# Decay tables by scaled exponentials, one table laid out row by row, and an operand split moved two products ahead

## The chip, the cores and the metric

One core of a Trainium2 chip runs the whole program. The metric is the device time of one execution in microseconds (us). Before the change it is 964.85 us, the median of 3 runs (964.2 to 965.12).

## What is computed

A block with adaptive layer norm: a modulation of a condition vector `c` scales and shifts two layer norms and gates two branches. The first branch is a long convolution whose kernel `K` is a sum of decaying complex exponentials (a diagonal state-space model), the second a bilinear gated unit. There are 2048 tokens, 640 channels `D`, 192 states `N` per channel, and 1536 hidden units `F`.

```python
logdA = dt * (A_re + 1j * A_im)
P = exp(logdA[:, :, None] * arange(L))          # D x N x L
K = einsum("dn,dnl,dn->dl", Cc, P, dt * Bc).real
y = irfft(rfft(pad(h)) * rfft(pad(K)))[:L] + h * Dskip
x = u + ga * y
h = layernorm(x) * (1 + cb) + sb
out = x + gb * (((h @ w_gate) * (h @ w_up)) @ w_down)
```

## The kernel before

**Stage 1 (about 0 to 430 us)** makes `K`, transforms it and the tokens, multiplies the spectra and transforms back. The 640 channels are taken in five blocks of 128. `K` is never summed term by term over `L`: an exponential at position `l` is a product of one at a coarse and one at a fine position, so for each of 40 groups (eight to a block, `n` = 0 to 39) the matrix engine multiplies a table of fine positions `P` with a table of coarse positions `Q` (L745 and L760). Each table is an amplitude times a sine or cosine. The amplitudes are `EP` (decay over fine positions) and `EQ` (decay over coarse ones, with the amplitude of the state), each an outer product that GpSimd (POOL) makes in `outer` (L649): `EP` from eight fine decays `LP` and four of the rows `RH`, `EQ` from eight values `LQ` and eight of the rows `RH`. GpSimd also makes the phases `Pha` and `Phb` on the same line. ScalarE (ACT) takes their sines into PSUM (`tra`, `trb`), and VectorE (DVE) multiplies these with `EP` and `EQ` on L731 (`PtA`, `PtB` read `EP`; `QtA`, `QtB` read `EQ`). `EP` and `EQ` have two buffers each, so that an outer product waits until the multiplication by the one before last has ended.

The decays come from a row of seeds for each block, one log decay per state, which TensorE transposes into PSUM (`ps`). The steps of a block's seeds stand in `u_seeds`, and the strings `SEG0` (first block) and `SEG` (the other four) say in which order they are recorded. Three of them matter here. `s_r` (L518) multiplies the log decay with constants: VectorE writes three multiples into `RL` (L521) and eleven into `RH` (L523), in two halves of a block. `s_e` (L535) takes exponentials on ScalarE: seven instructions with a scale of 64, 128, ... 448 write the fine decays `LP`, one runs over `RH` and one over `RL` in place. All ScalarE work goes through the helper `act` and has the line L135. `LP` is stored with the eight fine positions of a state side by side, so that each of the seven instructions writes every eighth element.

Beside the tables, the same engines do the transforms: `u_pre`, `u_g`, `u_c`, `u_d` for the tokens, the spectra, their product (L868 to L874 on VectorE) and the way back.

**Stage 2 (about 430 us to the end)** is the gated unit in two halves of the tokens. For each half, twelve steps `f` form gate and up products (`prod`, L1028) with sums of operands in the manner of a fast matrix multiplication; `y_3` and `z_2` are the last two products of a step, and VectorE, GpSimd and ScalarE combine their results. Every operand is split by `hilo` (L992) into a high part (ScalarE) and the remainder (VectorE). Then `down` (L1455) multiplies with `w_down` in twelve steps; `d_prep(tb, f)` splits that step's operands, `e` or `sl` on the token side and `wsgh`, `wsgl` on the weight side. The first two of these splits are recorded in the up loop itself, at the ends of steps 10 and 11.

**The order of the work** is written out by hand: the kernel runs under a manual schedule, each engine executes its instructions in the order in which they are recorded, and the table `SCHED` gives each piece of stage 1 the slots at which its parts are recorded. `q` in it are the slots of the seeds of the blocks after the first, one for each part of `SEG`. In stage 2 the Python loops are the order.

Of the kernel before, what the change touches and what calls it, by code (L numbers as in the profile page):

```python
# [10 lines left out]
F32 = mybir.dt.float32  # L11
F32R = mybir.dt.float32r
I32 = mybir.dt.int32
AF = mybir.ActivationFunctionType
OP = mybir.AluOpType
# [23 lines left out]
    fo=(22003, 31003, 31005, 35001),  # L39
    e0=(-87000,),  # L40
    mc=((31004, 39005, 40006, 43001, 52000), (34000, 53002, 60000, 62000, 69002), (58000, 91004, 92001)),
    q=((22004, 32000, 39001, 40005, 42006, 44000, 44001, 44002, 51000, 51001, 56001, 56002, 57000, 57002), (66002, 89000, 95003, 101000, 107000, 107001, 111000, 112000, 123000, 123003, 124001, 131000, 131003, 131004), (137001, 175000, 176001, 186009, 188001, 189001, 197003, 197004, 201000, 201001, 203002, 204001, 204002, 206001), (210002, 226000, 252005, 264003, 265002, 268001, 268002, 268003, 268005, 272001, 275000, 277000, 280002, 281001)),
    pre=(((56000, 73001, 78000), (40007, 61001, 66003), (76004, 82000, 86001), (88001, 95001, 97002)), ((119002, 127004, 132000), (131002, 131005, 135002), (86005, 99001, 100000), (118000, 118003, 118005)), ((143001, 160000, 160003), (153002, 172001, 172003), (181000, 186005, 186007), (173000, 178000, 178001)), ((221001, 252001, 252006), (224002, 242001, 242004), (245001, 261000, 261001), (281002, 281005, 285000)), ((317000, 335000, 336003), (265003, 298000, 298001), (297000, 315001, 315002), (182002, 196000, 196001))),
    c=(((161005, 162006, 165000, 166001), (122000, 122002, 154000, 155002), (144001, 144002, 167002, 168004), (125000, 125002, 141001, 141002)), ((208003, 217002, 220007, 224000), (201002, 201003, 205000, 211000), (181001, 181002, 198000, 200001), (168003, 170002, 184001, 186003)), ((292002, 295005, 308002, 308006), (245002, 249000, 253002, 253003), (254006, 256002, 278002, 281004), (291000, 291006, 302001, 303000)), ((319002, 321001, 329000, 332001), (337001, 337008, 346000, 349002), (351000, 351001, 360000, 364002), (363002, 365005, 365009, 370000)), ((375000, 379000, 391000, 392004, 393000, 403000), (386001, 386002, 392000, 393001, 394000, 404000), (380002, 385001, 388005, 392001, 392002, 392003), (365006, 371002, 392005, 396000, 398000, 404001))),
    d=(((376000, 388003, 388004), (206000, 206003, 210000), (222000, 225000, 225001), (283001, 284003, 291002)), ((236000, 244002, 248001), (251001, 261002, 262001), (267001, 270000, 270002), (224004, 240000, 244001)), ((340000, 358000, 358001), (354000, 367000, 367002), (319004, 338000, 339005), (309002, 325001, 332000)), ((397001, 401001, 409000), (406000, 414001, 414002), (402000, 414000, 431011), (411000, 424000, 431009)), ((404002, 406001, 407000, 412002), (409002, 412001, 419000, 419001), (425001, 425002, 429000, 431003), (404003, 409001, 415000, 415001))),
# [27 lines left out]
    xs='ababaaaabababa',  # L73
)
SEG0 = ("l", "a", "b", "c", "ud", "r", "x", "e", "f", "G", "g", "D", "h", "v", "R", "")
SEG = ("l", "a", "b", "c", "ud", "D", "r", "R", "x", "E", "f", "g", "h", "v")
P_PH, P_EP, P_MOD = 3, 6, 1


# [50 lines left out]
def tile_kernel(ctx: ExitStack, tc: tile.TileContext, I, out):  # L130
# [3 lines left out]
    def act(o, i, f=AF.Copy, **kw):  # L134
        return S.activation(o, i, f, **kw)  # L135
# [13 lines left out]
    sm = const.tile([P, 16], F32, name="sm")  # L149
    halfpi, dt, dt2 = sm[:, 10:11], sm[:, 0:NB], sm[:, NB : 2 * NB]  # L150
    V.memset(halfpi, math.pi / 2)
    mults = const.tile([P, 14], F32, name="mults")
    for k, m in enumerate((1536, 1024, 512, 0, 8, 16, 24, 32, 40, 48, 56, 1, 2, 4)):
        V.memset(mults[:, k : k + 1], float(m))
    shl = const.tile([P, 11], I32, name="shl")
    for k in range(11):
        V.memset(shl[:, k : k + 1], k + 1)
# [257 lines left out]
    EQ = [pk1.tile([P, 24, 64], F32, name=f"EQ{i}") for i in range(2)]  # L415
    EP = [pk1.tile([P, 24, 32], F32, name=f"EP{i}") for i in range(2)]
    LQ = pk1.tile([P, 96, 8], F32, name="LQ")
    LP = pk1.tile([P, 3, 96, 8], F32, name="LP")
    LH = pk1.tile([P, 192, 8], I32, name="LH")
    V.memset(LP[:, :, :, 0], 1.0)  # L420
    RH = pk1.tile([P, 3, 11, 96], F32, name="RH")
    RL = pk1.tile([P, 2, 4, 96], F32, name="RL")
    DH = [pk1.tile([P, 4, 192], I32, name=f"DH{i}") for i in range(3)]
    DL = [pk1.tile([P, 4, 192], I32, name=f"DL{i}") for i in range(2)]
# [3 lines left out]
    def u_seeds(db):  # L428
# [10 lines left out]
        dc = dt[:, db : db + 1]  # L439
        hs = (slice(0, 4), slice(4, 8))  # L440
        Dh, Dl = ([R[(2 * db + h) % len(R)] for h in range(2)] for R in (DH, DL))
        Rh, Rl = ([R[:, (2 * db + h) % R.shape[1]] for h in range(2)] for R in (RH, RL))

        def halves(R, hh):

            a, b = ((2 * db + h) % R.shape[1] for h in (hh[0], hh[-1]))
            return R[:, a : a + len(hh)] if a <= b else R[:, 2::-2]
# [14 lines left out]
        def free(h, *kinds):  # L462

            hf = 2 * db + h
            for k_ in kinds:
                if k_ in ("ph", "ep", "eq") and hf >= 3:
                    need(1, k_, 4 * (hf - 3) + 3)
                elif k_ in ("lh", "lq") and hf >= 2:
                    need(1, k_, hf - 2)
# [46 lines left out]
            mark("step", 2 * db + h)  # L516

        def s_r(h):  # L518
            ps = T["ps"]
            free(h, "ep", "eq", "lq")  # L520
            V.tensor_tensor(g4(Rl[h])[:, 0:3], ps[:, 0, hs[h]].unsqueeze(1).to_broadcast([P, 3, 4, 24]),  # L521
                            mults[:, 11:14].unsqueeze(2).unsqueeze(3).to_broadcast([P, 3, 4, 24]), op=OP.mult)
            V.tensor_tensor(g4(Rh[h]), ps[:, 0, hs[h]].unsqueeze(1).to_broadcast([P, 11, 4, 24]),  # L523
                            mults[:, 0:11].unsqueeze(2).unsqueeze(3).to_broadcast([P, 11, 4, 24]), op=OP.mult)

        def s_u():
            V.tensor_tensor(u, u, T["q"][:, 0], op=OP.add)
# [5 lines left out]
            V.tensor_scalar(pe[:, 1], x, 0.0, 0.5, op0=OP.is_ge, op1=OP.subtract)  # L533

        def s_e(*hh):  # L535
            lp, rh, rl = (halves(R, hh) for R in (LP, RH, RL))
            for l in range(1, 8):
                act(lp[:, :, :, l], rl[:, :, 0], AF.Exp, scale=64.0 * l)
            act(rh, rh, AF.Exp)
            act(rl[:, :, 0:3], rl[:, :, 0:3], AF.Exp)  # L540
            for h in hh:
                mark("lp", 2 * db + h)

# [34 lines left out]
        def s_v():  # L578
# [8 lines left out]
            for h in range(2):  # L587
# [1 line left out]
            mark("seeds", db)  # L589

        one = lambda f, *a: lambda: f(*a)
        steps = dict(l=s_l, a=s_a, b=s_b, c=s_c, d=one(s_d, 0), D=one(s_d, 1), r=one(s_r, 0), R=one(s_r, 1), u=s_u, x=s_x,
                     e=one(s_e, 0), E=one(s_e, 0, 1), f=s_f, G=s_G, g=s_g, h=s_h, v=s_v)
        if db == 0:
            LATE.append(lambda: s_e(1))
# [929 lines left out]
    for half in range(2):  # L1525
        i0 = half * NF
        if half == 0:

            new_s()
            new_h2()  # L1530
            H = iter(T0["hd"])
            seq = [(sums_u, 0), (x_1, 2), (x_2, 2, False), (x_c, 2), (split_u, 0, "a"), (split_u, 0, "b")]
            seq += [(tokens2, 1, 1, 0, False), (tokens2, 1, 1, 2, True), (s_sums, 0), (tokens2, 1, 1, 1, False), (tokens2, 1, 1, 3, False), (s_sums, 1)]
            seq += [(tokens2, 1, 1, 4, False), (x_1, 3), (x_2, 3, False)]
            seq += [(s_split, k, j) for j in (2, 1) for k in range(2)] + [(s_one, 4), (split_u, 0, "c"), (s_split, 0, 3), (s_split, 1, 3)]
            seq += [(s_one, 2), (s_one, 3), (s_split, 0, 4), (s_split, 1, 4), (s_five,), (x_c, 3), (sums_u, 1), (raw,), (raw_u, 2), (res_l, 0, 1)]
            seq += [(y_1, 0), (split_g, AHEAD), (z_1, 0), (y_2, 0), (split_u, 1), (sums_u, 2), (raw_u, 3), (y_3, 0), (z_2, 0), (fold, 0)]
            for g_, *a_ in seq:
                at((next(H),), once(g_), *a_)
            due(433)  # L1540
            assert not jobs
            PRE[0] = False
        else:
            for j in range(AHEAD):
                if LEAD <= j + 1 < AHEAD:
                    split_g(i0 + j + 1)
                x_1(i0 + j)
                x_2(i0 + j)
# [12 lines left out]
            res_l(3, 1)
        for f in range(1 - half, NF):
            i = i0 + f
            y_1(i)
            if f + AHEAD < NF:
                split_g(i + AHEAD)
            z_1(i)
            late = 0 < f <= NF - AHEAD
            if late:
                x_1(i + AHEAD - 1)  # L1570
            y_2(i)
            if f + 1 < NF:
                split_u(i + 1)
            if f + 2 < NF:
                sums_u(i + 2)
            if f + 3 < NF:
                raw_u(i + 3)
            if late:
                x_2(i + AHEAD - 1)
            y_3(i)  # L1580
            z_2(i)
            if half == 0:
                fold(f)
            if f >= NF - 2:
                d_prep(2 * half, f - NF + 2)
        for T in range(2):
            tb = 2 * half + T
            h2 = tb + 2 if half == 0 else None
            for f in range(NF):
                for n in (2, 3) if T == f == 0 else (f + LEAD,):  # L1590
                    if n < NF:
                        d_prep(tb, n)
                    elif T == 0:
                        d_prep(tb + 1, n - NF)
                    elif h2:
                        split_g(n)
# [26 lines left out]
```

## Time and profile before

| | |
|---|---|
| median of 3 runs | 964.85 us (964.2 to 965.12) |
| the profiled execution | 960.78 us, span 959.0 us, mean granted TensorE clock 0.978 |
| busy: PE, DVE, ACT, POOL | 863.3, 757.6, 569.7, 566.6 us |
| of these from 11.48 to 418.46 us (407.0 us): PE, DVE, ACT, POOL | 334.1, 353.4, 350.7, 385.9 us |

The profile is of one execution. Busy time is the time in which an engine had an instruction of the program in its datapath. A group row gives the line, the engine, the operation, the written and read tiles with their shapes, how many there were, their busy time and mean, and the idle time ahead of them with what ended it. A timeline row starts with start and length in us; a number in square brackets is the idle time of the engine before it, and the arrow what ended that. Ends of matrix multiplications are modelled, and ends of GpSimd work are rough.

### The profile page before, as it was taken

What the parts mean: (1) busy time and instruction counts of PE and PEld (TensorE: products, weight loads), DVE (VectorE), ACT (ScalarE), POOL (GpSimd) and SP (SyncE); (2) the same over time, 40 slices, a digit from 0 to 9 for tenths busy, and PEclk for the clock granted to TensorE, in tenths of its full rate; (3) what the DMA queues carried; (4) which work ended last, traced back from release to release, by engine and by line L of the source; (5) the groups of instructions that cost most, each with busy time, mean ns of one, the idle gap of its engine ahead of it and who ended that gap; (6) DMA issues with size and microseconds to landing.
All of it is one profiled execution on the core that took longest, in us unless ns stands there. A gap on an engine that the chain in (4) does not pass through costs nothing.

```text
span 959.0 us, 26424 instructions
## 1 busy us (share of the span) xinstructions
PE 863.3 (90%) x11070; PEld 715.4 (75%) x11070; DVE 757.6 (79%) x1328; ACT 569.7 (59%) x1022; POOL 566.6 (59%) x419
## 2 busy tenths in 40 slices
PE   2878876898798689889889999999999999999998
PEld 1565655676675467678568888889998888889998
DVE  8998688888889988888899777786677877687452
ACT  6899988887987879754773322225555322223330
POOL 5999999799799999940135866721021544451000
PEclk9977999999999899999999999999999999999999
DMA  8487575434455655478854355155536222212241
GB/s 304 150 289 243 164 222 194 138 112 129 139 183 157 178 148 159 126 228 245 234 157 121 99 192 180 40 192 165 193 137 219 84 83 82 83 55 84 82 166 55
DMA packets 141320, 148.94 MB, mean 155 GB/s; under 512 B 8208, under 2 KB 119568, under 8 KB 139792
## 3 DMA queue, kind: packets, MB, share of 16 engines
q1 hardware_dynamic: 139904, 145.80, 48.4%
q8 instruction: 87, 1.43, 0.6%
q10 hardware_dynamic: 1296, 1.44, 0.5%
q14 instruction: 33, 0.27, 0.1%
HBM read 108.36 MB, written 38.86 MB: 154 GB/s over the span
## 4 chain that ended last, share of the span: by engine, by line
PE 46%; DVE 6%; issue 1%; ACT 1%; POOL 1%; DMA 0%; SPq 0%; DVEq 0%; ACTq 0%
PE pa L1028 26%; PE pa L1455 17%; PE psg L1028 1%; DVE sl L992 1%; DVE wtl L992 0%; PE psg L1108 0%; DMA TVb<-WD 0%; PE psg L1455 0%; DVE a L1147 0%; DVE wsgl L992 0%; ACT hfb L135 0%; PE psg L1162 0%; DVE st L1081 0%; DVE xb L1468 0%; DVE hl L1149 0%
## 5 line engine op out<-in xcount | busy, mean ns | idle before, releaser
L649 POOL TENSOR_TENSOR EQ<-LQ,RH 128x1536 f32<-128x1536 f32 x40 | 124.1, 3103 | 1.1 <-DVE QtB L731 1.1
L135 ACT ACTIVATE z<-pa 128x512 f32<-128x512 f32 x24 | 14.3, 598 | 167.6 <-PE pa L1028 114.7
L992 DVE TENSOR_TENSOR wsgl<-wga,wsgh 128x640 fp32r<-128x640 f32 x72 | 67.6, 943 | 46.5 <-ACT wsgh L135 46.5
L135 ACT ACTIVATE wsgh<-wga 128x640 fp32r<-128x640 f32 x72 | 52.3, 732 | 66.5 <-PE pa L1455 30.2
L1399 POOL TENSOR_TENSOR z<-z,s 128x512 f32<-128x512 f32 x24 | 33.4, 1390 | 88.6 <-DVE s L1398 88.6
L1004 POOL TENSOR_TENSOR tf<-wur,wgb 128x256 f32<-128x256 f32 x24 | 18.8, 782 | 99.6 <-DVE wtl L992 58.9
L649 POOL TENSOR_TENSOR EP<-LP,RH 128x768 f32<-128x768 f32 x40 | 65.7, 1650 | 11.6 <-DVE PtB L731 11.5
L1455 PE MATMUL pa<-wsgh,sh 128*128 128x384 f32 (+1 forms) x295 | 68.6, 311 | 0.0
L1455 PE MATMUL pa<-wsgl,sh 128*128 128x384 f32 (+1 forms) x295 | 68.2, 310 | 0.0
L1455 PE MATMUL pa<-wsgh,sl 128*128 128x384 f32 (+1 forms) x295 | 68.2, 310 | 0.0
L649 POOL TENSOR_TENSOR Pha<-LH,DH 128x1536 int32<-128x1536 int32 (+1 forms) x21 | 62.4, 2971 | 1.3 <-ACT tra L135 1.1
L649 POOL TENSOR_TENSOR Phb<-LH,DH 128x1536 int32<-128x1536 int32 x20 | 62.2, 3112 | 0.0
L992 DVE TENSOR_TENSOR wtl<-tf,wth 128x256 fp32r<-128x256 f32 (+1 forms) x72 | 58.8, 843 | 0.0
L731 DVE TENSOR_TENSOR QtA<-tra,EQ 128x1024 f32<-128x1024 f32 x44 | 51.8, 1214 | 8.0 <-POOL LQ L643 3.2
L1397 DVE TENSOR_TENSOR s<-pa,s 128x512 f32<-128x512 f32 x24 | 16.6, 690 | 42.9 <-PE pa L1028 37.9
L731 DVE TENSOR_TENSOR QtA<-trb,EQ 128x1024 f32<-128x1024 f32 x36 | 42.7, 1215 | 9.6 <-ACT trb L135 3.9
L760 PE MATMUL kg<-QtB,PtB 64*32 64x64 f32 x2560 | 45.3, 220 | 4.3 <-issue 2.2
L760 PEld LDWEIGHTS kg<-QtB,PtB 64*32 64x32 f32 x2560 | 38.4, 108 | 11.8 <-issue 5.9
L1028 PE MATMUL pa<-sh,wtl 128*128 128x512 f32 x144 | 44.6, 391 | 0.9 <-DVE wtl L992 0.9
L1455 PEld LDWEIGHTS pa<-wsgh,sl 128*128 128x128 f32 x295 | 45.3, 188 | 0.0
L1455 PEld LDWEIGHTS pa<-wsgh,sh 128*128 128x128 f32 x295 | 45.3, 188 | 0.0
L1455 PEld LDWEIGHTS pa<-wsgl,sh 128*128 128x128 f32 x295 | 45.3, 188 | 0.0
(653 smaller groups left out, 2854.5 us busy)
## 6 DMA issues: line engine op xcount, KB each, us to landing
wga<-wdg SPq DMA_DIRECT2D x24, 640.0 KB, 4.3
wga<-B_w_gate SPq DMA_DIRECT2D x12, 640.0 KB, 5.9
wgb<-B_w_gate SPq DMA_DIRECT2D x24, 320.0 KB, 3.3
wur<-B_w_up SPq DMA_DIRECT2D x24, 320.0 KB, 4.0
xb<-x2d SPq DMA_DIRECT2D x6, 1280.0 KB, 8.6
t_ti<-w_mod SPq DMA_DIRECT2D x3, 1600.0 KB, 8.6
t_tw<-w_mod SPq DMA_DIRECT2D x3, 1600.0 KB, 9.5
WD<-Wa SPq DMA_DIRECT2D x8, 512.0 KB, 3.7
```

Of the source, the lines that this page charges most:

```text
L135: return S.activation(o, i, f, **kw)
L649: G.tensor_tensor(o.rearrange("p x (h l) -> p x h l", l=8), lo.unsqueeze(2).to_broadcast([P, rows, nh, 8]), hi.rearrange("p h x -> p x h") ...
L731: V.tensor_tensor(t, tr, e.unsqueeze(1).to_broadcast([P, 2, R, 32]), op=OP.mult)
L760: PE.matmul(kg[j * 32 : j * 32 + 32, dd, :], PtB[lo : lo + 64, c, r, :], QtB[lo : lo + 64, c, r, :], start=False, stop=dd == 7 and c == 1, ...
L992: V.tensor_tensor(lo, v, hi, op=OP.subtract)
L1004: G.tensor_tensor(t[:, 0:2], u[:, 0:2], g[:, 0:2], op=OP.subtract)
L1028: PE.matmul(ps, w[a][:, k], x[b][:, l], start=n == 0 and m == 0, stop=n == 2 and m == len(ks) - 1)
L1397: V.tensor_tensor(S67[i], ps, S6[i], op=OP.add)
L1399: G.tensor_tensor(ZT[i], ZT[i], S67[i], op=OP.add)
L1455: PE.matmul(ACC[tb][t][c], x[:, ts], w[:, cs], start=st, stop=f == NF - 1 and n == 2 and (one or t % 2 == 1))
```

## The change

It has two parts that do not touch each other.

The first is in stage 1. `s_r` no longer multiplies by constants: it copies the log decay once into row 0 of `RL`, for both halves of a block in one instruction (`S`; in the first block in two, `r` and `R`). `s_e` makes every decay directly, as an exponential of this row with a constant scale: seven for `LP`, ten for `RH`, three for `RL`, the last of them in place. Row 3 of `RH`, whose exponent is 0, is set to 1 once at the start. The tile of constants `mults` goes. `LP` is stored the other way round, eight rows of 96 states, so that ScalarE writes it side by side, and `mk_ep` hands GpSimd a view of it in the old order, in which neighbouring elements lie 96 elements (384 bytes) apart. The waits for the readers of the old `RH` move from `s_r` to `s_e`.

The second is in stage 2: in step 11 of each half the split for the second down step is recorded ahead of `y_3` and `z_2` and no longer behind them.

On VectorE, in the fourth block's seeds (`psfa` is the bank with the transposed log decay). Before:

```order
L731 TENSOR_TENSOR PtAa<-trb,EP_143 128x1024
L521 TENSOR_TENSOR RL<-psfa,mults 128x288
L523 TENSOR_TENSOR RH<-psfa,mults 128x1056
L521 TENSOR_TENSOR RL<-psfa,mults 128x288
L523 TENSOR_TENSOR RH<-psfa,mults 128x1056
L731 TENSOR_TENSOR PtB<-tra,EP_143 128x512
L731 TENSOR_TENSOR QtB<-tra,EQ_141 128x16x32 x2
```

With the change:

```order
L733 TENSOR_TENSOR PtAa<-trb,EP_128 128x1024
L520 COPY RL<-psfa 128x2x96
L733 TENSOR_TENSOR PtB<-tra,EP_128 128x512
L733 TENSOR_TENSOR QtB<-tra,EQ_126 128x16x32 x2
L529 TENSOR_SCALAR psfc<-ptb 128x192
```

Four instructions ahead of `PtB` became one. On ScalarE, in the same block's `s_e`, before:

```order
L135 ACT_TABLE_LOAD
L135 ACTIVATE LP<-RL 128x192 x7
L135 ACTIVATE RH<-RH 128x2112
L135 ACTIVATE RL<-RL 128x2x288
L135 ACT_TABLE_LOAD
```

With the change:

```order
L135 ACT_TABLE_LOAD
L135 ACTIVATE LP<-RL 128x2x96 x7
L135 ACTIVATE RH<-RL 128x2x96 x10
L135 ACTIVATE RL<-RL 128x2x96 x3
L135 ACT_TABLE_LOAD
```

Nine instructions became twenty, at the same place. On VectorE in step 11 of the first half (the `s` are the results of the up products, L1416 and L1405 those of `y_3` and `z_2`). Before:

```order
L1398 TENSOR_TENSOR s_8714<-z,s_8714 128x512
L1416 TENSOR_TENSOR s_8735<-psg,s_8735 128x512
L1405 TENSOR_TENSOR s_8714<-psg,s_8714 128x512
L1410 TENSOR_TENSOR a_7468<-a_7468,s_8714 128x512
L992 TENSOR_TENSOR e<-a_7456,e 128x512
L992 TENSOR_TENSOR wsgl<-wga,wsgh 128x640
```

With the change:

```order
L1400 TENSOR_TENSOR s_8752<-z,s_8752 128x512
L994 TENSOR_TENSOR e<-a_7494,e 128x512
L994 TENSOR_TENSOR wsgl<-wga,wsgh 128x640
L1418 TENSOR_TENSOR s_8773<-psg,s_8773 128x512
L1407 TENSOR_TENSOR s_8752<-psg,s_8752 128x512
L1412 TENSOR_TENSOR a_7506<-a_7506,s_8752 128x512
```

The pair of splits moved ahead of three combinations. On TensorE, GpSimd and SyncE no instruction moves, and on ScalarE none besides those of `s_e`.

```diff
-SEG = ("l", "a", "b", "c", "ud", "D", "r", "R", "x", "E", "f", "g", "h", "v")
+SEG = ("l", "a", "b", "c", "ud", "D", "S", "x", "E", "f", "g", "h", "v")
...
-    mults = const.tile([P, 14], F32, name="mults")
-    for k, m in enumerate((1536, 1024, 512, 0, 8, 16, 24, 32, 40, 48, 56, 1, 2, 4)):
-        V.memset(mults[:, k : k + 1], float(m))
...
-    LP = pk1.tile([P, 3, 96, 8], F32, name="LP")
+    LP = pk1.tile([P, 3, 8, 96], F32, name="LP")
     LH = pk1.tile([P, 192, 8], I32, name="LH")
-    V.memset(LP[:, :, :, 0], 1.0)
     RH = pk1.tile([P, 3, 11, 96], F32, name="RH")
+    V.memset(LP[:, :, 0], 1.0)
+    V.memset(RH[:, :, 3], 1.0)
...
         def s_r(h):
-            ps = T["ps"]
-            free(h, "ep", "eq", "lq")
-            V.tensor_tensor(g4(Rl[h])[:, 0:3], ps[:, 0, hs[h]].unsqueeze(1).to_broadcast([P, 3, 4, 24]),
-                            mults[:, 11:14].unsqueeze(2).unsqueeze(3).to_broadcast([P, 3, 4, 24]), op=OP.mult)
-            V.tensor_tensor(g4(Rh[h]), ps[:, 0, hs[h]].unsqueeze(1).to_broadcast([P, 11, 4, 24]),
-                            mults[:, 0:11].unsqueeze(2).unsqueeze(3).to_broadcast([P, 11, 4, 24]), op=OP.mult)
+            for i in h:
+                free(i, "lq")
+            rl = RL[:, 0:2, 0].rearrange("p h (s r) -> p h s r", r=24)[:, h[0] : h[-1] + 1]
+            V.tensor_copy(rl, T["ps"][:, 0, hs[h[0]].start : hs[h[-1]].stop].rearrange("p (h s) r -> p h s r", s=4))
...
         def s_e(*hh):
+            for h in hh:
+                free(h, "ep", "eq")
             lp, rh, rl = (halves(R, hh) for R in (LP, RH, RL))
             for l in range(1, 8):
-                act(lp[:, :, :, l], rl[:, :, 0], AF.Exp, scale=64.0 * l)
-            act(rh, rh, AF.Exp)
-            act(rl[:, :, 0:3], rl[:, :, 0:3], AF.Exp)
+                act(lp[:, :, l], rl[:, :, 0], AF.Exp, scale=64.0 * l)
+            for k in (2, 1, 0):
+                act(rh[:, :, k], rl[:, :, 0], AF.Exp, scale=512.0 * (3 - k))
+            for k in range(4, 11):
+                act(rh[:, :, k], rl[:, :, 0], AF.Exp, scale=8.0 * (k - 3))
+            for k in (2, 1, 0):
+                act(rl[:, :, k], rl[:, :, 0], AF.Exp, scale=float(2**k))
...
-        outer(EP[n % 2], LP[:, hf % 3, r], RH[:, hf % 3, 3::-1, r], 24, 4, OP.mult)
+        outer(EP[n % 2], LP[:, hf % 3, :, r].rearrange("p l x -> p x l"), RH[:, hf % 3, 3::-1, r], 24, 4, OP.mult)
...
+            if f == NF - 1:
+                d_prep(2 * half, 1)
             y_3(i)
             z_2(i)
             if half == 0:
                 fold(f)
-            if f >= NF - 2:
-                d_prep(2 * half, f - NF + 2)
+            if f == NF - 2:
+                d_prep(2 * half, 0)
```

In the table `SCHED`, the row `q` loses one slot for each of the four later blocks, since `S` takes the place of `r` and `R`.

More of the change, by code (lines that the diff above doesn't have):

```diff
@@ L41 @@
     mc=((31004, 39005, 40006, 43001, 52000), (34000, 53002, 60000, 62000, 69002), (58000, 91004, 92001)),
-    q=((22004, 32000, 39001, 40005, 42006, 44000, 44001, 44002, 51000, 51001, 56001, 56002, 57000, 57002), (66002, 89000, 95003, 101000, 107000, 107001, 111000, 112000, 123000, 123003, 124001, 131000, 131003, 131004), (137001, 175000, 176001, 186009, 188001, 189001, 197003, 197004, 201000, 201001, 203002, 204001, 204002, 206001), (210002, 226000, 252005, 264003, 265002, 268001, 268002, 268003, 268005, 272001, 275000, 277000, 280002, 281001)),
+    q=((22004, 32000, 39001, 40005, 42006, 44000, 44001, 51000, 51001, 56001, 56002, 57000, 57002), (66002, 89000, 95003, 101000, 107000, 107001, 111000, 123000, 123003, 124001, 131000, 131003, 131004), (137001, 175000, 176001, 186009, 188001, 189001, 197003, 201000, 201001, 203002, 204001, 204002, 206001), (210002, 226000, 252005, 264003, 265002, 268001, 268002, 268005, 272001, 275000, 277000, 280002, 281001)),
     pre=(((56000, 73001, 78000), (40007, 61001, 66003), (76004, 82000, 86001), (88001, 95001, 97002)), ((119002, 127004, 132000), (131002, 131005, 135002), (86005, 99001, 100000), (118000, 118003, 118005)), ((143001, 160000, 160003), (153002, 172001, 172003), (181000, 186005, 186007), (173000, 178000, 178001)), ((221001, 252001, 252006), (224002, 242001, 242004), (245001, 261000, 261001), (281002, 281005, 285000)), ((317000, 335000, 336003), (265003, 298000, 298001), (297000, 315001, 315002), (182002, 196000, 196001))),
@@ L441, in u_seeds @@
         Dh, Dl = ([R[(2 * db + h) % len(R)] for h in range(2)] for R in (DH, DL))
-        Rh, Rl = ([R[:, (2 * db + h) % R.shape[1]] for h in range(2)] for R in (RH, RL))
+        Rl = [RL[:, h] for h in range(2)]
         def halves(R, hh):
@@ L591, in u_seeds @@
         one = lambda f, *a: lambda: f(*a)
-        steps = dict(l=s_l, a=s_a, b=s_b, c=s_c, d=one(s_d, 0), D=one(s_d, 1), r=one(s_r, 0), R=one(s_r, 1), u=s_u, x=s_x,
+        steps = dict(l=s_l, a=s_a, b=s_b, c=s_c, d=one(s_d, 0), D=one(s_d, 1), r=one(s_r, (0,)), R=one(s_r, (1,)), S=one(s_r, (0, 1)), u=s_u, x=s_x,
                      e=one(s_e, 0), E=one(s_e, 0, 1), f=s_f, G=s_G, g=s_g, h=s_h, v=s_v)
```

## The prediction, made before the run

> **What bounds the kernel now.** I read the page first for the span, then the busy time by stretch and the waits of GpSimd in the stretch that the first part of the change touches, and then the chain of work that ended last.
>
> ```profile
> span 959.0 us, 26424 instructions
> core 0: us, PE busy (x) PEld busy (x) DVE busy (x) ACT busy (x) POOL busy (x), PEclk, DMA share, GB/s
> 11.48:418.46 406.98, 334.13 (x7494) 252.71 (x7496) 353.36 (x575) 350.65 (x610) 385.90 (x240) 0.95 0.57 177
> ```
>
> From GpSimd's first table work (11.48) to the end of its last amplitude table (418.46) GpSimd is busy for 385.9 of 407.0 us, 95%. VectorE and ScalarE are at 87% and 86%, TensorE at 82%. So whatever leaves VectorE in this stretch leaves an engine that has 54 us to spare, and whatever lands on GpSimd lands on one that has 21. Its waits there, with the three long ones by place:
>
> ```profile
> POOL EP L649 <- DVE PtB L731: 11.5, 3, 6.3
> POOL Pha L649 <- ACT tra L135: 1.1, 1, 1.1
> POOL EQ L649 <- DVE QtB L731: 1.1, 1, 1.1
> POOL LQ L643 <- DVE RL L571: 0.9, 2, 0.5
> POOL DL L585 <- POOL ptb L584: 0.7, 1, 0.7
> ...
> 173.78 1.65 POOL L649 TENSOR_TENSOR EP<-LP,RH 128x768 f32<-128x768 f32 x1 [4.37 <-DVE PtB L731]
> ...
> 252.42 1.66 POOL L649 TENSOR_TENSOR EP<-LP,RH 128x768 f32<-128x768 f32 x1 [6.27 <-DVE PtB L731]
> ...
> 333.94 3.26 POOL L649 TENSOR_TENSOR EP<-LP,RH 128x768 f32<-128x768 f32 x2 [0.89 <-DVE PtB L731]
> ```
>
> That is 15.3 us of real waiting, 10.6 of it at two places, both ended by VectorE freeing an `EP` buffer. The other 6 us or so are gaps between instructions, which come with their number. After the stage TensorE sets the end:
>
> ```profile
> 638.09 41.92 PE pa L1455 x284
> ...
> 870.57 45.05 PE pa L1455 x307
> ```
>
> These are two of the long pieces of the chain; from 638 us on it is almost nothing but such pieces. What shifts the end of stage 1 shifts the start of this, and so the end, one for one.
>
> **The change part by part.** *VectorE's multiples.* They leave, and a copy comes.
>
> ```profile
> L523 DVE TENSOR_TENSOR RH<-psfa,mults x6: 1244/1244/1244, 147.2 to 331.7; 128x1056 f32<-128x1056 f32 x6
> L521 DVE TENSOR_TENSOR RL<-psfa,mults x6: 444/444/444, 146.8 to 331.3; 128x288 f32<-128x288 f32 x6
> L571 DVE COPY RL<-psfa x4: 247/252/256, 92.6 to 339.9; 128x96 f32<-128x96 f32 x4
> ```
>
> A later block had two pairs, 2 x (1.24 + 0.44) = 3.38 us. The first two rows give 1.04 ns an element, so the copy of 192 takes about 0.25 + 0.10 = 0.35 (an estimate from the copy of 96). That frees 3.03 us in each of four blocks, and 2 x (1.69 - 0.25) = 2.9 in the first: 15.0 us of VectorE. It reaches GpSimd only where GpSimd waits behind these instructions. That is one place above all, the wait of 6.27 us, where the freeing `PtB` stands right behind the four instructions:
>
> ```profile
> 251.60 0.68 DVE L731 TENSOR_TENSOR PtB<-tra,EP 128x512 f32<-128x512 f32 x1
> ...
> 249.38 0.60 ACT L135 ACTIVATE tra<-ab 128x512 f32<-128x512 f32 x1
> ```
>
> The `PtB` could start 3.0 us earlier, but it reads the cosine that ScalarE ends at 249.98. So it gains 1.6 us, not 3.0; ScalarE is late next. At 173.78 the four instructions are over 20 us back, and VectorE has waited for ScalarE in between: I take nothing there.
>
> *ScalarE's exponentials.* Nine instructions become twenty. Rows of one later block:
>
> ```profile
> 162.83 0.36 ACT L135 ACTIVATE ptb<-ptb 128x192 f32<-128x192 f32 x1
> 163.10 0.32 ACT L135 ACTIVATE psfc<-ptb 128x192 f32<-128x192 f32 x1
> ...
> 164.72 2.70 ACT L135 ACTIVATE LP<-RL 128x192 f32<-128x192 f32 x7
> ...
> 169.07 0.67 ACT L135 ACTIVATE RL<-RL 128x576 f32<-128x576 f32 x1
> ```
>
> The old set took from 164.72 to 169.74, 5.02 us. Side by side, 192 elements follow each other after 0.27 us, so twenty take 19 x 0.27 + 0.36 = 5.5: +0.5 us a later block. Writing `LP` side by side pays for most of the eleven more. In the first block's two sets the same eleven cost at most 11 x 0.27 = 3.0 us each, less what the shorter `RH` saves; GpSimd has other tables to make then. ScalarE is not the fullest engine and I take 0 of this for the path; uncovered it is up to 4 x 0.5 = 2 us from the later blocks. The wait for the readers of the old `RH` moves from VectorE's queue to ScalarE's, ahead of the sines queued there; there are three rings of `RH`, the readers ended half a block earlier, and no row shows VectorE waiting for them. Nothing.
>
> *GpSimd's strided read.* No instruction is added, but 40 of them read `LP` in another way, and this is the largest term.
>
> ```profile
> L649 POOL TENSOR_TENSOR EP<-LP,RH 128x768 f32<-128x768 f32 x40 | 65.7, 1650 | 11.6 <-DVE PtB L731 11.5
> ...
> L634 POOL TENSOR_TENSOR LH<-LH,DL 128x192 int32<-128x192 int32 x9 | 6.2, 690 | 0.7
> L628 POOL TENSOR_TENSOR DH<-DH 128x192 int32<-128x192 int32 x9 | 5.3, 593 | 0.0
> ...
> L609 POOL TENSOR_TENSOR LQ<-LQ,RL 128x192 f32<-128x192 f32 x10 | 5.6, 559 | 0.8
> ```
>
> L634 and L628 are the same size. L628 reads two operands side by side; L634 reads one of its two at every eighth element, 32 bytes apart. The difference is 97 ns over 192 elements, 0.5 ns an element. L609 reads one operand in side-by-side pairs that lie 32 bytes apart and writes with that jump too, at 559: a jump at every second element costs nothing visible. `EP` after the change jumps 384 bytes at every element, like L634 and unlike L609. So the price of the jump is 768 x 0.505 = 0.39 us, `EP` 2.04 us, 40 of them +15.5 us. Bounds: nothing (+0), if the broadcast second operand of `EP`, which L634 does not have, leaves room for it; and 768 x 690/192 = 2.76 us at most, +44 us, if the whole of L634 with its fixed part counted by element, which is too much. A more sensible upper end adds half as much again, 0.6 us each, +24. I take 0.39, the difference of the nearest pair.
>
> [...]
>
> How much of +15.5 us reaches the end depends on where the tables stand between the waits:
>
> ```profile
> 11.48:92.99 81.51, 11.24 (x12) 13.12 (x8) 0.85 0.73 254
> 92.99:173.78 80.79, 14.85 (x16) 11.46 (x7) 0.98 0.57 181
> 173.78:252.42 78.64, 15.18 (x16) 11.53 (x7) 1.00 0.48 138
> 252.42:333.94 81.52, 15.10 (x16) 13.14 (x8) 0.94 0.57 167
> 333.94:418.46 84.52, 16.36 (x17) 16.46 (x10) 0.98 0.49 143
> ```
>
> (The second bracket is the number of `EP` made in each stretch.) The first three stretches hold 22, +8.6 us, against about 2.7 + 4.4 + 6.3 = 13.4 us of waits. These waits take it all. At 252.42 GpSimd leaves when `PtB` frees the buffer, 1.6 us earlier by the above, less what the later tables have cost VectorE on the way, which I put at 0.7: -0.9. The last two stretches hold 18, +7.0 us, against 0.9 + 1.1 us of waits: +5.0. Sum for GpSimd at its end: +4.1 us. Its readers have a little slack there:
>
> ```profile
> 406.01 3.11 POOL L649 TENSOR_TENSOR EQ<-LQ,RH 128x1536 f32<-128x1536 f32 x1
> ...
> 410.56 2.36 DVE L731 TENSOR_TENSOR QtA<-tra,EQ 128x1024 f32<-128x1024 f32 x2 [0.48 <-ACT Wa L135]
> ```
>
> That table ends at 409.12 and is read at 410.56, 1.4 us, and two `EP` (0.8 us) still come after it. So VectorE's last stretch, which ends the stage, is later by 4.1 - 2.2 = **+1.9 us**.
>
> *The split moved ahead.* At the first `down` of the first half:
>
> ```profile
> 634.08 0.69 DVE L1416 TENSOR_TENSOR s<-psg,s 128x512 f32<-128x512 f32 x1 [1.41 <-POOL z L1399]
> ...
> 636.62 0.68 DVE L992 TENSOR_TENSOR e<-a,e 128x512 fp32r<-128x512 f32 x1
> 637.22 0.81 DVE L992 TENSOR_TENSOR wsgl<-wga,wsgh 128x640 fp32r<-128x640 f32 x1
> ...
> 637.35 0.56 PE L1455 MATMUL pa<-wsgh,e 128*128 128x384 f32 x2 [0.91 <-DVE e L992]
> 638.09 0.56 PE L1455 MATMUL pa<-wsgl,e 128*128 128x384 f32 x2 [0.17 <-DVE wsgl L992]
> ```
>
> TensorE waits 0.91 and 0.17 us for the pair. The pair takes about 1.35 us from start to end of the datapath and now fits into the 1.41 us in which VectorE waited for GpSimd's `z`, so L1416 and what is queued behind it keep their time. Gain 0.91 + 0.17 = **-1.1 us**. In the second half no row shows TensorE waiting there: 0. If VectorE's idle time were not there, three combinations would be 1.4 us later, and no product reads them soon.
>
> **Sum:** +1.9 - 1.1 = +0.8 us on the span of 959.0. The profiled execution took 960.78 us and the median is 964.85, 4.1 above it; I carry the change over: 965.7, said as **966 us**.
>
> **The rivals.** *The strided read is free* (for it: L609's pairs and the broadcast operand; against it: L634). Then GpSimd leaves 252.42 with -1.6, loses the waits of 0.9 and perhaps 1.1 behind it, and the stage ends 2.5 to 3.6 us earlier; with -1.1 that is 960 to 961.5 us, faster.
>
> *GpSimd's read costs more and rules the stage* (slower side): at 0.6 us each the first three stretches have 13.2 us against 13.4, the last two 10.8 - 2.0 = +8.8, less 1.4 + 1.2 of slack, less 1.1: +5.1, 970 us. For it: a jump of 384 bytes is wider than L634's 32. It decides from where the price passes 0.45 us. [...]
>
> *ScalarE is late next.* At 249.38 it already holds up VectorE; +0.5 us in four blocks on the path, and the first block's, add 2 to 3 us: 968 to 969. Against it: its 86%.
>
> **How the numbers follow.** No change can be told from this measurement within 0.2%, 1.9 us. My forecast 0.45, with a range of its own of 963 to 969, since the 0.7 and the slack can be off by 2 or 3 us (faster 0.04, same 0.24, slower 0.17). Free read 0.30 (faster 0.28, same 0.02). Dearer read 0.17, of it 0.05 for the rule's size. ScalarE 0.08 (same 0.03, slower 0.05). Together faster 0.32, same 0.29, slower 0.39. The range of 959 to 973 reaches over the free read and over the middle of the dearer one.
>
> **What would show it.** The `EP` group's mean first: 2.04, or 1.65, or 2.3 and more. GpSimd's waits for `PtB` shrunk at 173.78 and 252.42, its busy time in the stretch up by 15 us. ScalarE's set of a later block at 5.5 us. TensorE's waits for `e` and `wsgl` at the first `down` gone. I am wrong if VectorE's 15 us show in the stage's length, or if `EP` keeps its mean and the stage is no shorter.

## The result

The changed kernel takes 971.2 us (median of 6 runs, 970.14 to 973.48), the kernel before 964.2 us beside it (6 runs, 962.89 to 965.12). The ratio is 1.0079, 95% interval 1.0063 to 1.0096: slower. 966 was forecast, with a range of 959 to 973 and 0.39 for slower. So the time lies in the range, but on the side of the rivals.

The profiled execution after took 970.89 us, span 969.1 us, against 960.78 and 959.0 before. GpSimd's groups and waits in stage 1 after the change (the same columns as in the prediction):

```profile
L651 POOL TENSOR_TENSOR EP<-LP,RH 128x768 f32<-128x768 f32 x40 | 83.8, 2101 | 4.8 <-DVE PtB L733 4.8
...
POOL EP L651 <- DVE PtB L733: 4.8, 2, 2.8
...
POOL LQ L645 <- DVE RL L573: 1.4, 1, 1.4
...
176.97 2.11 POOL L651 TENSOR_TENSOR EP<-LP,RH 128x768 f32<-128x768 f32 x1 [2.81 <-DVE PtB L733]
...
254.55 2.09 POOL L651 TENSOR_TENSOR EP<-LP,RH 128x768 f32<-128x768 f32 x1 [2.04 <-DVE PtB L733]
```

`EP` takes 2.10 us, 0.45 more; the waits for `PtB` fell from 11.5 to 4.8 us, but did not go. In their place other engines wait for GpSimd: VectorE for `EQ` and ScalarE for `Pha`. Before, VectorE has no wait for `EQ` at all and ScalarE this one for `Pha`:

```profile
ACT PtAb L135 <- POOL Pha L649: 4.3, 3, 2.1
```

After:

```profile
DVE QtA L733 <- POOL EQ L651: 7.0, 7, 2.4
...
ACT PtAb L135 <- POOL Pha L651: 8.1, 5, 3.2
```

This is no accident of one trace. In the four kernels of this document whose GpSimd makes all 40 `EP` at 2.10 us, ScalarE's wait is 7.5 to 10.1 us and VectorE's 5.0 to 10.0; in the eight that make them at 1.65, it is 3.5 to 4.6 and at most 2.1.

The place at 252.42 us, where VectorE's relief was to reach GpSimd, on ScalarE and VectorE after the change:

```profile
249.49 1.06 ACT L135 ACTIVATE PtAb<-Pha 128x1024 f32<-128x1024 int32 x1 [0.54 <-POOL Pha L651]
...
252.28 0.35 DVE L520 COPY RL<-psfa 128x192 f32<-128x192 f32 x1
253.72 0.69 DVE L733 TENSOR_TENSOR PtB<-tra,EP 128x512 f32<-128x512 f32 x1 [1.08 <-ACT tra L135]
```

The four multiples are one copy, and `PtB` now waits for the cosine, as forecast. But the cosine itself is late: `PtB` starts at 253.72 and not at 251.60. Ahead of it ScalarE waited for GpSimd's phases (`Pha`, at 249.49); that wait is 0.54 us, so it is only a part of the delay.

ScalarE's set of a later block, and TensorE at the first `down`:

```profile
167.91 1.88 ACT L135 ACTIVATE LP<-RL 128x192 f32<-128x192 f32 x7
169.69 2.62 ACT L135 ACTIVATE RH<-RL 128x192 f32<-128x192 f32 x10
172.22 0.99 ACT L135 ACTIVATE RL<-RL 128x192 f32<-128x192 f32 x3
...
641.04 0.68 DVE L994 TENSOR_TENSOR e<-a,e 128x512 fp32r<-128x512 f32 x1
641.64 1.92 DVE L994 TENSOR_TENSOR wsgl<-wga,wsgh 128x640 fp32r<-128x640 f32 x1
643.49 0.68 DVE L1418 TENSOR_TENSOR s<-psg,s 128x512 f32<-128x512 f32 x1
```

The set takes 5.3 us (167.91 to 173.21). The second pair of splits (641.04 and 641.64) runs ahead of L1418, and TensorE, which reaches its product at 644.7, has no wait there. The pair takes 2.5 us, though, and not the 1.35 of the prediction: `wsgl`, which now runs while GpSimd makes `z`, takes 1.92 us in place of 0.81.

What the forecast did not have at all stands in the last two stages. The chain of waits holds pieces of the same number of the same matmuls in both kernels, before (with the piece at 870.57 that the prediction shows) and after:

```profile
503.60 105.73 PE pa L1028 x465
...
726.76 139.73 PE pa L1028 x615
...
952.99 2.48 DVE xb L1468 x6
```

```profile
734.39 140.55 PE pa L1030 x615
...
879.02 45.92 PE pa L1457 x307
...
963.11 2.48 DVE xb L1470 x6
```

615 matmuls of the up loop, a mix of shapes, take 0.82 us longer, 1.3 ns each; 307 of `down` take 0.87 us longer, 2.8 ns each. The groups of `down` by shape say the same, before and after:

```profile
L1455 PE MATMUL pa<-wsgh,sl 128*128 128x384 f32 x148 | 50.0, 338 | 0.0
...
L1455 PE MATMUL pa<-wsgh,sl 128*128 128x256 f32 x139 | 38.8, 279 | 0.0
```

```profile
L1457 PE MATMUL pa<-wsgh,sl 128*128 128x384 f32 x147 | 50.1, 341 | 0.0
...
L1457 PE MATMUL pa<-wsgh,sl 128*128 128x256 f32 x140 | 39.5, 282 | 0.0
```

The granted clock is 1.00 in both from 640 us on. No line of the diff touches these instructions. What it does touch is the list of tiles: the table `mults`, 56 bytes a partition, is gone, and in the built program the tiles that are laid out behind it from the same end of the memory begin 64 bytes lower. `wsgh` began at byte 45536 of a partition, 96 over a multiple of 128, and begins at 45472, 32 over one; `wsgl` moves with it. `sh` and `sl` are laid out from the other end and keep their address. So in these groups only one operand has moved, the one that TensorE streams (`wsgh` or `wsgl`, 256 or 384 columns); the one of 128 by 128 that it holds has not. That became a theory of its own, beside two others: that GpSimd paces stage 1, so that the dearer read is paid; and that ScalarE's twenty exponentials are.

### The profile page after: what moved, and what is told of

It reads as the page before. It is cut to its first block, busy times and chain, and to the rows that moved or that the text cites. A ratio compares the mean times of both kernels' runs of the same rounds, so it can differ in the third digit from the quotient of the medians.

```text
span 969.1 us, 26463 instructions
## 1 busy us (share of the span) xinstructions
PE 867.6 (90%) x11070; PEld 718.8 (74%) x11070; DVE 747.2 (77%) x1301; ACT 573.0 (59%) x1088; POOL 585.4 (60%) x419
## 4 chain that ended last, share of the span: by engine, by line
PE 48%; DVE 4%; ACT 1%; issue 1%; DVEq 0%; ACTq 0%
PE pa L1030 28%; PE pa L1457 16%; PE psg L1030 1%; DVE st L1083 1%; DVE sl L994 1%; PE psg L1164 1%; PE psg L1110 0%; PE psg L1457 0%; PE psfc L829 0%; PE psfa L829 0%; DVE a L1149 0%; ACT hh L135 0%; PE psfb L829 0%; ACT xb L135 0%; DVE xb L1470 0%
## 5 line engine op out<-in xcount | busy, mean ns | idle before, releaser
L994 DVE TENSOR_TENSOR wsgl<-wga,wsgh 128x640 fp32r<-128x640 f32 x72 | 70.8, 987 | 47.4 <-ACT wsgh L135 47.4
L651 POOL TENSOR_TENSOR EP<-LP,RH 128x768 f32<-128x768 f32 x40 | 83.8, 2101 | 4.8 <-DVE PtB L733 4.8
```

What stands on the lines that cost most here:

```text
L651: G.tensor_tensor(o.rearrange("p x (h l) -> p x h l", l=8), lo.unsqueeze(2).to_broadcast([P, rows, nh, 8]), hi.rearrange("p h x -> p x h") ...
L994: V.tensor_tensor(lo, v, hi, op=OP.subtract)
```

## The experiments

Each run stands beside runs of the kernel before on the same chip. Those had medians of 964.2, 964.2, 964.1 and 962.6 us in the four groups of runs, and single runs scatter over 7 to 11 us. One trace is worse than a median for stage 1. In the trace of part 2 alone the code up to 500 us is that of before, word for word, and yet TensorE is 5 us later at that point. Four traces with the stage 1 of before come to it at 503.6, 505.7, 508.5 and 510.7 us. In this one the granted clock was 0.79 for 8 us, which may be a part of it. Before, and part 2 alone (TensorE, weight load, VectorE, ScalarE, GpSimd, then the clock):

```profile
432.00:440.00 8.00, 8.00 (x174) 7.48 (x168) 5.21 (x13) 5.43 (x11) 0.00 (x0) 1.00 1.03 330
```

```profile
432.00:440.00 8.00, 5.46 (x72) 3.79 (x73) 0.81 (x2) 2.32 (x5) 0.00 (x0) 0.79 0.89 301
```

From 503 us on, in contrast, traces of equal code agree within 0.1 us. So I take the part behind this point (503 us before, where the long piece of the up loop begins) from the traces, and stage 1 from the medians less that part.

**Each part alone, and the layout alone.** Part 2 alone moves `d_prep(2 * half, 1)` in the kernel before; part 1 alone leaves it where it was. Expected for part 2 alone:

> Part 2 alone on the kernel before. Pacemaker theory (GpSimd's table reads cost the time, part 2 saves what it was said to): TensorE's waits of 0.91 and 0.17 us for e and wsgl at the first down are gone, 964.2 - 1.1 to 1.3 = about 963.0 us. Rival (ScalarE theory) says nothing else of this part. If the move costs VectorE something later, 964 or more.

Measured 963.39 against 964.22 us, ratio 0.9989 (0.9966 to 1.0013): the median as expected, the interval holds no change as well. Its trace has 1.6 us less behind 503 us. For part 1 alone:

> Part 1 alone. Both theories: the 7.0 us of the whole change plus the 1.1 to 1.3 that part 2 gives, 964.2 + 8.2 = about 972.4 us, with EP at 2.10 us. If the two parts are not additive, it differs from this by more than 1 us.

971.41 us, ratio 1.0083 (1.0056 to 1.0109), 1 us under the expectation: the two parts add up within what can be measured.

Then the layout without the rest, and the rest without the layout:

```diff
-    LP = pk1.tile([P, 3, 96, 8], F32, name="LP")
+    LP = pk1.tile([P, 3, 8, 96], F32, name="LP")
...
-                act(lp[:, :, :, l], rl[:, :, 0], AF.Exp, scale=64.0 * l)
+                act(lp[:, :, l], rl[:, :, 0], AF.Exp, scale=64.0 * l)
...
-        outer(EP[n % 2], LP[:, hf % 3, r], RH[:, hf % 3, 3::-1, r], 24, 4, OP.mult)
+        outer(EP[n % 2], LP[:, hf % 3, :, r].rearrange("p l x -> p x l"), RH[:, hf % 3, 3::-1, r], 24, 4, OP.mult)
```

> Only the layout: LP row by row and read at the jump, with VectorE's old multiples and ScalarE's nine old instructions, no part 2. Pacemaker theory: EP at 2.10 us, GpSimd + 18 us less the waits that swallow some 10 to 13 of it: + 7 to + 10 us, 971 to 974 us. Rival (ScalarE): the waits of GpSimd swallow nearly all, ScalarE has nine instructions as before, 964 to 967 us.

969.09 us, ratio 1.0053 (1.0035 to 1.0071): 4.9 us for the layout, less than the theory's 7 and more than ScalarE's would have. `EP` took 2.10 us:

```profile
L649 POOL TENSOR_TENSOR EP<-LP,RH 128x768 f32<-128x768 f32 x40 | 83.7, 2102 | 5.8 <-DVE PtB L731 5.8
```

The whole change with these three lines turned back:

> The whole change, but LP keeps its old layout: ScalarE writes it at a jump of 32 bytes, GpSimd reads it side by side. Pacemaker theory: EP back at 1.65 us, 40 x 0.45 = 18 us leave GpSimd, VectorE's relief and part 2 are all that is left: stage 1 ends 2.5 to 3.6 us earlier than before, the whole 959 to 961 us. Rival (ScalarE is late next): ScalarE has all twenty exponentials and its set of a later block is longer still (some 6 us against 5.3), so the time stays at 968 to 972 us though EP is short.

967.9 us, ratio 1.0039 (1.0019 to 1.0059), though `EP` was back at 1.66 us. By the expectation that was ScalarE's theory, and it seemed to stand: its set took 6.0 us a block. To see it alone, the next run gave VectorE its multiples back (nobody reads them) and left ScalarE with the twenty:

> Only ScalarE's twenty exponentials in place of nine, LP in its old layout, VectorE still makes all multiples (nobody reads them), no part 2. Against the run with the old layout this gives VectorE its 15 us back. Theory 1 (VectorE's relief is worth nothing, ScalarE's longer set, 6.0 against 5.0 us, stands on the path): 967.9 + 0.8 for part 2 = 968 to 969.5 us. Theory 2 (VectorE's relief is worth the 2.5 to 3.6 us of the prediction, ScalarE costs all the more): 971 to 972.5 us. Theory 3 (ScalarE costs nothing, the old layout was slow for another reason): 964 us.

965.81 us, ratio 1.0018 (1.0000 to 1.0036). That fits none of the three, and is 2 us less than the run with the old layout, in which VectorE had 15 us less to do. A relief that costs time was the contradiction that led to the matmul rows: 338 ns here, where the table `mults` is still there, 341 ns in the run with the old layout, where it is gone.

**The addresses.** The whole change, with an unused tile of 64 bytes where the table lay:

```diff
+    pad = const.tile([P, 16], F32, name="pad")
+    V.memset(pad[:, 0:1], 0.0)
     shl = const.tile([P, 11], I32, name="shl")
```

> The whole change plus an unused tile of 64 bytes a partition where the table of multiples lay, so that every tile behind it has its old address again. Theory of addresses (the matmuls of the last stages that stream wsgh and wsgl take 282 and 341 ns in place of 279 and 338 in every kernel without the table, and in none with it): 279 and 338 ns again, 2.9 us of TensorE back, 971.2 - 2.9 = 968.3 us. Rival (those 3 ns come from the granted clock or from another part of the change): 282 and 341 ns stay, 971 us.

966.47 us, ratio 1.0018 (1.0000 to 1.0037), 4.7 us less than the change without the tile, where 2.9 were expected. Its rows have the old times:

```profile
L1459 PE MATMUL pa<-wsgl,sh 128*128 128x384 f32 x152 | 51.4, 338 | 0.0
...
732.56 139.75 PE pa L1032 x615
...
876.38 45.05 PE pa L1459 x307
...
958.80 2.48 DVE xb L1472 x6
```

And the other way round, in the kernel before: the same table, taken from another pool, so that the tiles of the last stages begin 64 bytes lower and the tables of stage 1 stay where they are. All instructions are those of before; the constants are written one place later.

```diff
-    mults = const.tile([P, 14], F32, name="mults")
+    mults = pk1.tile([P, 14], F32, name="mults")
```

> The kernel before, with nothing changed but the place of the table of multiples: it lies behind the constants, so that the tiles of the last stages (wsgh, wsgl and others) begin 64 bytes lower, as after the change, while LP, RH and the tables of stage 1 stay where they are. Theory of addresses: 282 and 341 ns for the matmuls that stream wsgh and wsgl, 2.9 us more, 967 us. Rival (the 64 bytes matter only together with the change): 279 and 338 ns, 964.1 us.

967.2 against 962.64 us, ratio 1.0061 (1.0037 to 1.0086). The rows:

```profile
L1455 PE MATMUL pa<-wsgh,sl 128*128 128x384 f32 x151 | 51.5, 341 | 0.0
...
505.66 106.51 PE pa L1028 x465
...
730.38 140.51 PE pa L1028 x615
...
874.97 45.92 PE pa L1455 x307
...
959.05 2.48 DVE xb L1468 x6
```

From the piece at 503.60 to the last combination: 952.99 - 503.60 = 449.4 us before, 959.05 - 505.66 = 453.4 us here. So 64 bytes cost 4.0 us, in a kernel whose arithmetic and order are untouched. This theory stands. A start on the 128-byte line itself was tried too, with an unused tile of 32 bytes and part 2:

> Part 2 alone plus an unused tile of 32 bytes a partition ahead of the others: wsgh and its neighbours then begin at a multiple of 128 bytes (before: 96 over one; after the change: 32 over one). Theory of addresses: the matmuls' time changes with it, and since the sign for this place is not known from any run, 279 ns or less and 963.4 us or less if a start on the 128-byte line is the best place, some 282 ns and 966.3 us if it is like 32 over. Rival (addresses do not matter): 279 ns and 963.4 us, nothing moved.

963.01 us, ratio 0.9991 (0.997 to 1.0012), not to be told from part 2 alone. The products of `down` take 279 and 336 ns, no more than before. Other products like this place less: in its trace the first 549 matmuls of the up loop take 125.76 us, against 124.98 in part 2 alone and 125.69 in the change, and the whole way behind 503 us is 448.7 us, 0.9 more than with part 2 alone. So the 128-byte line is no better place for all of them together.

**The read.** The whole change, in which GpSimd takes the eight rows as if they lay in the old order, and so the wrong elements:

```diff
-        outer(EP[n % 2], LP[:, hf % 3, :, r].rearrange("p l x -> p x l"), RH[:, hf % 3, 3::-1, r], 24, 4, OP.mult)
+        lp = LP[:, hf % 3].rearrange("p l x -> p (l x)").rearrange("p (x l) -> p x l", l=8)
+        outer(EP[n % 2], lp[:, r], RH[:, hf % 3, 3::-1, r], 24, 4, OP.mult)
```

> The whole change, but GpSimd reads the row-by-row LP as if it lay in the old order, side by side; this leaves the right choice of LP's elements out, and the time of the read alone is changed: EP back at 1.65 us. It is the world of the rival of the prediction, the free read. Theory 1 (GpSimd's 18 us cost what they cost alone, 5 us): 971.2 - 5 = about 966 us, of which 2.9 are the addresses. Theory 2 (ScalarE's set rules, as with the old layout): 968 to 971 us. The prediction's own price for this world: 971.2 less 5 to 6 us.

965.6 us, ratio 1.0018 (1.0004 to 1.0032): 5.6 us less than the change, all by the read. The first theory holds.

The read by itself, in a kernel of nothing else:

> A small kernel that leaves the whole computation out and only times reads, four of each, nothing beside them on the other engines: GpSimd's EP product of 768 elements with LP at a step of 4, 8, 16, 32 and 384 bytes, then with LP and RH taken row by row (24 side by side in both), with the result side by side and with a jump of 128 bytes; VectorE's product of 1024 with EP side by side and at a step of 96 bytes; ScalarE's exponential of 192 written side by side and at a step of 32 bytes. Theory 1 (the price is the jump itself, the same from 8 or 16 bytes up): 1.65 us at 4, 2.10 at all steps from 8 or 16 on. Theory 2 (the price grows with the distance): 1.65, then rising, with 32 bytes clearly under 2.10 and 384 at 2.10. Row by row on both sides: 1.65 if only the operand's jump counts. ScalarE 0.27 against 0.38 us a piece.

The tiles `step__69`, `step__74`, `step__79`, `step__84` and `step__89` are the steps of 4, 8, 16, 32 and 384 bytes, `rowsin__94` the product row by row. Some of the sums of VectorE that end the small kernel did run beside GpSimd, against the expectation's "nothing beside them". Rows with no VectorE beside them:

```profile
10.69 1.64 POOL L50 TENSOR_TENSOR step__69<-big,hi 128x768 f32<-128x768 f32 x1
12.29 1.66 POOL L50 TENSOR_TENSOR step__74<-big,hi 128x768 f32<-128x768 f32 x1
...
22.18 1.97 POOL L50 TENSOR_TENSOR step__79<-big,hi 128x768 f32<-128x768 f32 x1
24.11 2.00 POOL L50 TENSOR_TENSOR step__84<-big,hi 128x768 f32<-128x768 f32 x1
...
42.56 2.09 POOL L50 TENSOR_TENSOR step__89<-rows,hi 128x768 f32<-128x768 f32 x1
44.61 1.78 POOL L50 TENSOR_TENSOR rowsin__94<-rows,hi 128x768 f32<-128x768 f32 x1
```

A step of 8 bytes took 0.02 us more than one of 4 (1.66 against 1.64), one of 16 took 0.33 us more (20%), one of 384 took 0.45 more (27%): in these rows a cliff between 8 and 16 bytes and a slight slope behind it, so each theory had half. Row by row it took 1.78 us, where 1.65 was expected if only the operand's jump counts.

**VectorE's relief.** By the working of the prediction a free read was to bring 2.5 to 3.6 us, from VectorE's relief. Alone (copy for multiples, ScalarE with nine instructions on constants, the table kept):

> VectorE's relief alone: the copy in place of the multiples, ScalarE with its nine instructions in the old layout, the unused table kept for the addresses, no part 2. RH and the rest of RL are taken as constants (ScalarE exponentiates zero times their contents), so the powers are left out of the result; the instructions of stage 1 are otherwise as before. By the prediction's working, with EP unchanged the stage ends 2.5 to 3.6 us earlier: 960.5 to 961.6 us. Ring theory (the old layout against the exponentials alone gave 0.0 us once 2.9 us for the addresses and 0.8 us for part 2 are taken out): within 1 us of 964.1.

963.62 against 962.64 us, ratio 0.9997 (0.9975 to 1.0018): nothing that can be measured, and the forecast gain lies outside the interval. GpSimd sets the constants first, so its tables begin 0.3 us later here. Its waits show where the relief went:

```profile
POOL EP L651 <- DVE PtB L733: 10.6, 3, 5.9
...
POOL LQ L645 <- DVE RL L573: 3.4, 3, 1.9
POOL Pha L651 <- ACT tra L135: 2.1, 1, 2.1
```

The waits for `PtB` gave up 0.9 us (11.5 before), those for the next amplitudes grew by 2.5 (0.9 before) and for a `tra` by 1.0 (1.1 before). In the three other traces with the stage 1 of before, these are 11 to 13, 1.3 to 1.6 and 0.8 to 1.0 us, so the two that grew are clear of the scatter. GpSimd reaches the amplitudes sooner than they are ready: VectorE's copy of them (`RL`, L573) itself waits 3.7 us for TensorE in this trace.

**Products moved to VectorE.** A try for a faster kernel: if GpSimd paces the stage and VectorE has room, 11 `EP` belong on VectorE.

> Part 2 alone, with 11 of the 40 EP products made by VectorE in place of GpSimd (old layout, old multiples). VectorE's price is estimated at 0.86 us each (768 elements at 1.04 ns and some 0.06), + 9.5 us for VectorE, - 18 us for GpSimd. Theory 1 (GpSimd paces stage 1, VectorE has room): 2 to 4 us less than part 2 alone, 959.5 to 961.5 us. Theory 2 (stage 1 hangs on a ring of all engines, and what one sheds is waited for at the next): 963 us. Theory 3 (VectorE's queue is in the way): 965 us or more.

973.55 us, ratio 1.0098 (1.0074 to 1.0123), 10 us more than part 2 alone, as the third theory has it. My price was wrong: not 0.86 but 1.48 us each, from 0.95 to 2.38.

```profile
L649 DVE TENSOR_TENSOR EP<-LP,RH 128x768 f32<-128x768 f32 x11 | 16.3, 1482 | 0.0
...
143.50 0.95 DVE L649 TENSOR_TENSOR EP<-LP,RH 128x768 f32<-128x768 f32 x1
202.18 2.38 DVE L649 TENSOR_TENSOR EP<-LP,RH 128x768 f32<-128x768 f32 x1
```

VectorE got 16 us more, put into a queue on which every product waits. So its 54 us to spare are not there when they are wanted, and 16 us more cost much where 15 us less had brought nothing.

No kernel that was tried beats the one before by more than the measurement tells. Part 2 alone takes 1.6 us less by its trace, under a fifth of a per cent.

## Why the prediction was right and wrong

The medians put together, each as the difference to the kernel before on its chip (us). The middle column is by the method of the address run, from the beginning of the long piece of the up loop (503 us before) to the last combination.

| run | whole | behind 503 us, by the trace | stage 1, the rest |
|---|---|---|---|
| the change | +7.0 | +2.4 | +4.6 |
| part 1 alone | +7.2 | +4.0 | +3.2 |
| the change, old addresses | +2.4 | -1.6 | +4.0 |
| layout alone | +4.9 | 0 | +4.9 |
| the change, read side by side | +1.5 | +2.4 | -0.9 |
| the change, old layout | +3.7 | +2.4 | +1.3 |
| VectorE's relief alone | +1.0 | 0 | +1.0 |
| exponentials alone, old layout | +1.6 | 0 | +1.6 |
| part 2 alone | -0.8 | -1.6 | +0.8 |
| before, shifted by 64 bytes | +4.6 | +4.0 | +0.6 |

The last two have the stage 1 of before, and should read 0 in the last column; they read 0.8 and 0.6. The intervals of the ratios are wider, 1.3 to 2.5 us to either side of each row, so differences of 1 or 2 us between single rows tell nothing.

- *The read.* Forecast 2.04 us an `EP`, measured 2.10; forecast 4.4 to 5.5 us of time between the free read and the dear one, measured 4.6 + 0.9 = 5.5 between the change and the read side by side. This step held: the nearest pair of rows said 0.39 us an `EP`, the upper end of half as much again 0.6, and 0.45 was measured. The 0.05 that went to "the rule's size" stood for a still dearer read, which no run shows: the dear read added 27%, 2.10 us against 1.65. There is luck in it: L634 not only reads but also writes at every eighth element, which the prediction passed over, so the difference to L628 was not the price of a read alone.
- *VectorE's relief.* "It gains 1.6 us" at 252.42, 2.5 to 3.6 us in all with a free read. Measured: nothing alone, and 0.9 us with ScalarE's change, which is within the scatter. The step that failed is that GpSimd leaves this place 0.9 us earlier. The release is no fixed date. It hangs on a cosine, the cosine on ScalarE's queue, and that queue on GpSimd's own phases, which ended 3.6 us before the cosine began. In the trace GpSimd left it 2.1 us later, with 2.04 us of wait still there. One trace can't fix that figure, as traces with the stage 1 of before leave the place anywhere from 252.4 to 255.0 us; what all traces of the dear read show are the longer waits of ScalarE and VectorE for GpSimd. GpSimd's waits for `PtB` shrank by 6.7 us, while the 22 `EP` of the first three stretches grew by 9.9 (22 x 0.45). So these waits did not take the first 8.6 us whole either, and stage 1 ended some 4 us later (3.2 to 4.6 in the three runs), not 1.9.
- *ScalarE's set.* Forecast 5.5 us, measured 5.3 in the change. With the old layout it is 6.0, and the longer set alone costs some 1.6 us (0 to 3.5), so that its rival was not wholly wrong for that layout. Writing `LP` side by side takes 0.27 us a piece against 0.38, as the working said.
- *Part 2.* Forecast -1.1, by the trace -1.6; the waits for `e` and `wsgl` are gone. The pair did not fit into VectorE's 1.41 us, as it takes 2.5 us beside GpSimd, but TensorE did not wait for it.
- *The end.* "What shifts the end of stage 1 shifts the start of this, and so the end, one for one": here the sum broke. It took the later stages as they were, and they grew by 4.0 us, since a table that leaves moves the tiles behind it. With the old addresses the change takes 966.5 us, 2.4 more than the kernel before (0 to 3.6), where 0.8 was forecast: the 2 us that stage 1 takes more than forecast, and half a us back by part 2. That run alone would not contradict the forecast.

The change was forecast at +0.8 us and measured at +7.0. Of the 6.2 us between them, 4.0 had no term and 2.7 are stage 1, with 0.5 back from part 2. That 971 still lies in the range of 959 to 973 is luck as far as the 4.0 go: the range was made wide for other reasons. The rival of the dearer read was forecast at 970, near the measured 971, and was still the wrong story: its 0.6 us an `EP` was 0.45.

What stays open is what in the address of the streamed operand costs TensorE the 3 ns in `down`. There 384 columns of `wsgh` with `sl` took 341 ns at 32 bytes over a multiple of 128, 336 at 0 and 338 at 96 over; 64 over was not tried. In the up loop both operands of some products move, and which of them counts was not taken apart.

## What to carry to other kernels

A diff has a part that it doesn't show, the addresses (64 bytes cost 4.0 us here): when a tile goes or changes its size, compare the duration of untouched instructions by shape, before and after, ahead of any story on waits; an unused tile of the same size tells the two apart in one run. A wait is room only if the one who ends it doesn't hang on the one who waits; follow the releaser back two or three steps before you let a wait swallow a cost. And traces of the same code differed by up to 7 us in stage 1 here, so a difference of 0.5% wants code that is equal up to a point as a yardstick.

## What the runs showed of the hardware

- Matmuls that stream `wsgh` and `wsgl` against an `sh` or `sl` that keeps its address take 282 and 341 ns for 256 and 384 columns where the streamed tiles begin 32 bytes over a multiple of 128, 279 and 338 at 96 over, 279 and 336 at 0. (The group of `wsgh` with `sh` has 344, 341 and 339 for 384 columns.) That was not expected.
- GpSimd's product of 768 elements: 1.64 us at a step of 4, 1.66 at 8, 1.97 at 16, 2.00 at 32, 2.09 at 384 bytes.
- VectorE reading its second operand at a step of 96 bytes takes 2.69 us for 1024 elements, against 1.22 side by side, with GpSimd idle:

```profile
L65 DVE TENSOR_TENSOR ptrows__112<-tr,rowsin__94 128x1024 f32<-128x1024 f32 x4 | 10.8, 2690 | 0.1
L65 DVE TENSOR_TENSOR ptside__107<-tr,step__69 128x1024 f32<-128x1024 f32 x4 | 4.9, 1224 | 0.1
```

  That is 2.6 ns an element against 1.2, with one operand at the step. It speaks against a table `EP` laid out row by row, which was not tried in the whole kernel.
- Some instructions of VectorE and GpSimd that ran at the same time took longer than without each other. In the small kernel GpSimd's product at 16 bytes took 2.55 us beside VectorE's sums and 1.97 without, and such a sum of 640 elements 2.40 us beside GpSimd and 0.82 alone:

```profile
17.14 2.55 POOL L50 TENSOR_TENSOR step__79<-big,hi 128x768 f32<-128x768 f32 x1
...
17.96 2.40 DVE L78 TENSOR_TENSOR acc<-acc,step__74 128x640 f32<-128x640 f32 x1
...
59.24 0.82 DVE L78 TENSOR_TENSOR acc<-acc,rowsout__99 128x640 f32<-128x640 f32 x1
```

  With the change the split `wsgl` took 1.92 us beside GpSimd's `z`, and `z` 1.68; before, where they did not run together, they took 0.81 and 1.29. Whether GpSimd is also why `EP` on VectorE took up to 2.38 us was not tried apart.
